# Turns of PSUM banks, mirrored value products and a new order of pairs in a fused attention and feed-forward kernel

## The chip, the cores and the metric

The kernel runs on one core of one Trainium2 chip. The time is the device time of one execution in microseconds (us). A number called "time" is the median of the undisturbed executions of one kernel; each batch of measurements ran the kernel before on the same chip in between. A number from a trace comes from one profiled execution and is counted from the start of its span.

Engines: PE is TensorE's matmuls, PEld its weight loads, DVE is VectorE, ACT is ScalarE, POOL is GpSimd. PSUM is the memory that TensorE writes its results to; the kernel uses it as a tile `ps` of eight banks of 512 columns. `xT` is the normalised result of attention, transposed, the input of stage 1. "L584" is line 584 of the kernel that was profiled, so one statement has different line numbers in different kernels.

## The reference

```python
# q, k, v: (8 batches, 8 heads, 576 tokens, 64); per head, softmax over a causal band
mask_plain = (rel >= 0) & (rel < 32)                          # heads 0..3
mask_dil = (rel >= 0) & (rel < 128) & (rel % 4 == 0)          # heads 4..7 ("dilated"; heads 0..3 are "plain")
attn = exp(scores - max) / (sum + 1e-09); attn_out = attn @ v
x = attn_out.transpose(0, 2, 1, 3).reshape(4608, 512)
g, val = x @ w_gate, x @ w_val                                # 512 -> 1536
out = (gelu(g) * val) @ w_out                                 # 1536 -> 512, fp32
```

## The kernel before

The 4608 tokens go through the feed-forward part in nine pieces (c = 0 to 8) of 512. Each piece has two stages. Stage 1 makes 12 pairs of PSUM banks, one for the gate and one for the values; ScalarE takes the gelu of the first, VectorE multiplies. Stage 2 makes four output blocks of 128 tokens, each the sum of 12 products in one bank, and ScalarE stores them. Attention is worked off two heads (a "pair" of heads, index n = 4 x batch + pair) at a time in between: scores (s), mask (m), value product (v), and the multiply by the reciprocal of the denominators (x); w is the last value product of a stage, in the banks of the scores. The string `places` says where each of these steps comes: "1.3v" is a value product in output block 1, counted from 0, after three of its twelve products.

ScalarE needs the exponential for the scores and gelu for stage 1. In the trace of the kernel before, each of the 13 changes between the two comes with a load of tables of 1283 ns (seven for gelu, six for the exponential). No source line asks for it: the compiler puts it in.

```python
    def ffn1_two(c, pairs):              # first two bank pairs of a piece
        for kc in range(NKC):            # NKC = 4: one kc for each pair of heads
            for nb in range(2):
                ...                      # gate and value product of this kc
        for nb in range(2):
            geglu(nb, pairs[nb])

    def geglu(nb, b0):
        g = ffn.tile([P, CH], F16, tag="g")        # a pool of three g buffers
        nc.scalar.activation(g, ps[:, b0, :], AF.Gelu)
        nc.vector.scalar_tensor_tensor(u_all[:, nb, :], g, USCALE, ps[:, b0 + 1, :], ALU.mult, ALU.mult)
    ...
    places = {
        1: "0.0m 1.2v 1.2x 1.2s 1.2m 1.12s 2.1v 2.1x 2.1m 2.12s 3.1v 3.1m 3.1x 3.12w 3.12x",
        ...                              # pieces 2 to 5
    }
    ...
            for tb in range(4):          # stage 2
                ...
                bank = mm0 + tb if not lone else first if tb == 0 else mm0
                ffn2(c, tb, bank, hooks)
                store(c, tb, bank, "dve" if c > 5 and tb == 3 else "act")
```

Scores take four of the eight banks, so a stage 2 with attention in it has the other four at hand (`mm0` to `mm0 + 3`): blocks 1 to 3 all use the bank `mm0`, so blocks 2 and 3 have to wait until ScalarE has stored the one before (2.2 us from 85 to 260 us, in seven waits of up to 0.3).

The softmax here doesn't subtract the row's maximum and nothing guards it: scores larger than these inputs give would overflow.

Of the kernel before, what the change touches and what calls it, by code (L numbers as in the profile page):

```python
# [17 lines left out]
USCALE = 32.0  # L18
# [20 lines left out]
def kernel(  # L39
# [211 lines left out]


    def is_plain(n):
        return n % NHP < NHP // 2

# [126 lines left out]

    def emit_pv(n, b0, parts=("den", "num"), wide=False):

# [16 lines left out]
        if is_plain(n):  # L401
            if "den" in parts:
                d0 = 1024 if wide else 960

                groups = (
                    ((0, 0, 4, P), (P, P, 3, 32), (PH - PT, 512, 1, PT))
                    if wide
                    else ((0, 0, 1, 64), (64, 64, 1, 64), (PW, P, 3, P), (P, P, 3, 32), (PH - PT, 512, 1, PT))
                )
                for i, (p0, q0, runs, w) in enumerate(groups):  # L410
                    for hl in range(2):
                        st = i == 0 or i == (2 if wide else 1)
                        add(hl, d0 + q0, [[P, runs], [1, w]], ones[:, 0:D], hl * PH + p0, [[PW, runs], [1, w]], st)
            if "num" in parts:
                for j in range(5):
                    for hl in range(2):
                        lhs = vp[:, j, hp, 2 * hl, :] if j < 4 else vt[:, hp, 2 * hl, :]
                        w = (PW, PW, PW, P, PT)[j]
                        add(hl, j * P, run(w), lhs, hl * PH + j * PW - (32 if j == 4 else 0), run(w), j in (0, 4))
        else:  # L420
            if "den" in parts:

                groups = (
                    ((0, 0, DW, 1024), (1, 0, DW, 1536))
                    if wide
                    else ((0, 0, 192, 288), (0, 192, 96, 800), (1, 0, 96, 896), (1, 96, 192, 1312))
                )
                for i, (s, c, w, c0) in enumerate(groups):
                    for hl in range(2):
                        add(hl, c0, run(w), ones[:, 0:D], (2 * s + hl) * DW + c, run(w), wide or i != 2)  # L430
            if "num" in parts:
                for s in range(2):
                    for m in range(3):
                        for hl in range(2):
                            h, p0 = 2 * hp + hl, (2 * s + hl) * DW
                            if m < 2:
                                add(hl, 512 * s + m * NCL, run(P), vd[:, h, 2 * m + s, :], p0 + m * NCL, run(P), m == 0)
                            else:
                                two = [[NCL, 2], [1, 16]]
                                add(hl, 512 * s + P, two, vr[:, h, s, :], p0 + P, two, False)  # L440
        for o, lhs, rhs, st in mms:
# [33 lines left out]
    def norm_both_x(n, b0):  # L475
        b, hp = divmod(n, NHP)
        rb = tiles.pop(("rb", n))
        for hl in range(2):
            half = slice(64 * hl, 64 * hl + 64)
            nc.vector.tensor_tensor(  # L480
                xT[hp][half, b * S : (b + 1) * S], both_rows(hl, b0, hl), rb[half], ALU.mult
            )

    def den_ap(n, b0, wide):

        if is_plain(n):
            c0, dims = (1024, [[1, S]]) if wide else (960, [[1, S]])
        else:
# [3 lines left out]

    def norm_r(n, b0, wide=False):
        dt = nrm.tile([P, 18, 32], F32, tag="dt", bufs=1)
        den = den_ap(n, b0, wide)
        dims = den.ap[1:]
# [5 lines left out]

    def recip(n, dt):
        rc = nrm.tile([P, 18], F32, tag="rc")
        nc.vector.reciprocal(rc, dt[:, :, 0:1].rearrange("p b c -> p (b c)"))
        rb = nrm.tile([P, S], F32, tag="rb", bufs=4)
        nc.vector.transpose(  # L507
            rb.rearrange("p (b c) -> p b c", c=32),
            bass.AP(tensor=rc.tensor, offset=rc.offset, ap=[rc.ap[0], [1, 18], [0, 32]]),
        )  # L510
        tiles["rb", n] = rb

    def norm_x(n, b0):
        b, hp = divmod(n, NHP)
        rb = tiles.pop(("rb", n))
        dst = xT[hp][:, b * S : (b + 1) * S]
        if is_plain(n):
            nc.vector.tensor_tensor(dst, psf[:, b0 * 512 : b0 * 512 + S], rb, ALU.mult)
        else:
            num = ps[:, b0 : b0 + 2, 0 : 2 * NCL].rearrange("p s (m i) -> p i m s", m=2)  # L520
            nc.vector.tensor_tensor(  # L521
# [5 lines left out]

    def ffn1(c, nb, b0):
        tok = slice(c * CH, (c + 1) * CH)
        ns = slice((nb % 4) * P, (nb % 4 + 1) * P)  # L530
        for gi, w in ((0, wg_t[nb // 4]), (1, wv_t[nb // 4])):
            for kc in range(NKC):
                nc.tensor.matmul(  # L533
                    ps[:, b0 + gi, :], w[:, kc, ns], xT[kc][:, tok], start=(kc == 0), stop=(kc == NKC - 1)
                )
        geglu(nb, b0)

    def ffn1_two(c, pairs):

        tok = slice(c * CH, (c + 1) * CH)  # L540
        for kc in range(NKC):
            for nb in range(2):
                ns = slice(nb * P, (nb + 1) * P)
                for gi, w in ((0, wg_t[0]), (1, wv_t[0])):
                    nc.tensor.matmul(  # L545
                        ps[:, pairs[nb] + gi, :],
                        w[:, kc, ns],
                        xT[kc][:, tok],
                        start=(kc == 0),
                        stop=(kc == NKC - 1),  # L550
                    )
        for nb in range(2):
            geglu(nb, pairs[nb])

    def geglu(nb, b0):
        g = ffn.tile([P, CH], F16, tag="g")
        nc.scalar.activation(g, ps[:, b0, :], AF.Gelu)  # L557
        nc.vector.scalar_tensor_tensor(u_all[:, nb, :], g, USCALE, ps[:, b0 + 1, :], ALU.mult, ALU.mult)  # L558

# [106 lines left out]
    for hp in range(2):  # L666
# [18 lines left out]


    places = {
        1: "0.0m 1.2v 1.2x 1.2s 1.2m 1.12s 2.1v 2.1x 2.1m 2.12s 3.1v 3.1m 3.1x 3.12w 3.12x",
        2: "0.0m 1.2v 1.2x 1.2s 1.2m 1.12s 2.1v 2.1x 2.1m 2.12s 3.1v 3.1x 3.1m 3.7s 3.12v 3.12x 3.12m",
        3: "0.0m 1.2v 1.2x 1.2s 1.2m 1.12s 2.1v 2.1x 2.1m 2.12s 2.12m 3.1v 3.1x 3.7s 3.7m",  # L690
        4: "0.0m 1.4s 1.12v 1.12x 1.12m 2.3s 2.12v 2.12x 2.12m 3.2s 3.2m 3.12s 3.12m",
        5: "0.0m 1.4s 1.4m 1.12v 1.12x 2.3s 2.3m 2.12s 2.12m 3.6s 3.6m",
    }
    places = {c: [(int(w[0]), int(w[2:-1]), w[-1]) for w in p.split()] for c, p in places.items()}
    late = None
    for c in range(NCH):
# [4 lines left out]
        s_list = list(scores.get(c, ()))  # L701
        pairs = (mm0, mm0 + 2)
        swap = int(c < 2 or late == "bank")
        SB = 4 - mm0
# [3 lines left out]
        for nb in range(NNB):  # L708
            if nb == 0 and c < 2:
                ffn1_two(c, (4, 6) if c == 0 else (6, 0))  # L710
            elif nb == 0 and late == "x":
                ffn1_two(c, pairs)
            elif nb > 1 or c > 2 and late != "x":
                ffn1(c, nb, pairs[(nb + swap) % 2])
            if pend is not None:
# [30 lines left out]

        def norm(n, b0):
            norm_r(n, b0)
            norm_x(n, b0)


        V = mm0 + 1

# [17 lines left out]
        else:  # L771
            todo = list(values_b.get(c, ()))
            lone = c in values_b
            first = pairs[(NNB - 2 + swap) % 2] + (pairs[(NNB - 2 + swap) % 2] == mm0)

            going = []

            def do(kind):
                if kind == "s":
# [3 lines left out]
                elif kind == "x":  # L783
                    norm_x(*going.pop(0))
                else:
                    n, bank = todo.pop(0), SB if kind == "w" else V
                    emit_pv(n, bank)
                    norm_r(n, bank)
                    going.append((n, bank))

            late = None
            for tb in range(4):
                at = [(fc, kind) for t, fc, kind in places.get(c, ()) if t == tb]
                hooks = {}
                for fc, kind in at:
                    if fc < NNB:
                        hooks.setdefault(fc, []).append(lambda kind=kind: do(kind))
                bank = mm0 + tb if not lone else first if tb == 0 else mm0
                ffn2(c, tb, bank, hooks)
                store(c, tb, bank, "dve" if c > 5 and tb == 3 else "act")  # L800
                for fc, kind in at:
                    if fc == NNB:
                        do(kind)
            if lone:

                late = "bank"
                if len(values_b[c]) > 2:
                    late = "x"
                    if c > 1:
                        mm0 = 4 - mm0  # L810
            while masks:
# [29 lines left out]
```

## Time and profile before

| | kernel before |
|---|---|
| time | 360.56 us (360.35 to 361.32, 4 runs) |
| span of the profiled run | 358.6 us |
| TensorE / VectorE / ScalarE busy | 95% / 56% / 41% |
| ScalarE's table loads for gelu | 7, of 1283 ns each |

The prediction shows how TensorE's waits are found. This is the timeline of the kernel before, at the change from piece 1 to piece 2. The columns of a timeline are the start (us), the duration (us), engine, line, operation, output<-input and shapes, count, and in brackets the idle time before it with what ended it.

```profile
105.69 0.60 ACT L575 ACTIVATE osb<-ps 128x512 f32<-128x512 f32 x1 [2.56 <-PE ps L564]
...
106.30 1.28 ACT L557 ACT_TABLE_LOAD   x1
...
110.24 1.09 ACT L557 ACTIVATE g<-ps 128x512 f16<-128x512 f32 x2 [2.66 <-PE ps L545]
...
110.89 1.02 PE L533 MATMUL ps<-xT,wg 128*128 128x512 f16 x4
```

The load runs at 106.30, right behind the last store (0.02 us after its end). ScalarE then stands 2.66 us until TensorE has the first gate bank ready. TensorE starts its third bank pair (L533) 0.65 after the gelu's start, only 0.20 us later than it could.

### The profile page before, as it was taken

How to read it: one execution, taken by the hardware profiler on the slowest of the kernel's cores; microseconds unless marked ns; L12 is line 12 of the kernel's file. 1: busy time of each engine (PE TensorE's matmuls, PEld its weight loads, DVE VectorE, ACT ScalarE, POOL GpSimd, SP SyncE). 2: the span in 40 equal slices, each digit the busy share in tenths (PEclk: the TensorE clock that was granted, in tenths of full speed). 3: DMA queues.
4: the chain of work that ended last, by engine and by line, in shares of the span. 5: the costliest groups of instructions: out<-in, count | busy, mean ns of one | idle time of the engine just before them, and what ended most of it. 6: DMA issues, size and time to landing. Idle time of an engine off the chain costs nothing.

```text
span 358.6 us, 5943 instructions
## 1 busy us (share of the span) xinstructions
PE 342.4 (95%) x2326; PEld 165.7 (46%) x2326; DVE 201.3 (56%) x306; ACT 145.3 (41%) x212; POOL 78.4 (22%) x110
## 2 busy tenths in 40 slices
PE   6789999999999999899999999999999999999995
PEld 2554454444444444344445444544454444444442
DVE  3575455843585447773768837993589514403320
ACT  1732346253643364435463366326643223323321
POOL 2580334540432323063003600140000000000000
PEclk9958999999999999999999999999999999999999
DMA  8999999999899899699139952794100020011002
GB/s 197 240 188 214 212 150 197 177 163 242 182 137 204 192 155 177 161 182 136 60 99 205 149 115 76 167 159 71 59 31 0 31 88 0 3 72 45 2 29 88
DMA packets 107291, 45.30 MB, mean 126 GB/s; under 512 B 83040, under 2 KB 102496, under 8 KB 107264
## 3 DMA queue, kind: packets, MB, share of 16 engines
q1 hardware_dynamic: 84272, 31.21, 39.9%
q0 software_dynamic: 21456, 12.01, 26.5%
q10 hardware_dynamic: 1536, 1.70, 2.1%
q8 instruction: 18, 0.29, 0.4%
q14 instruction: 9, 0.07, 0.1%
HBM read 40.13 MB, written 9.44 MB: 138 GB/s over the span
## 4 chain that ended last, share of the span: by engine, by line
PE 79%; DVE 11%; DMA 3%; ACT 3%; issue 2%; ACTq 0%; DVEq 0%
PE ps L533 42%; PE ps L564 24%; PE ps L442 5%; PE ps L545 4%; DMA xT<-in_k_dram 3%; DVE xT L521 2%; DVE dt L500 2%; DVE rb L507 2%; ACT osb L575 1%; DVE dt L470 1%; PE ps L339 1%; DVE u_all L558 1%; PE ps L369 1%; DVE xT L480 1%; DVE P L379 1%
## 5 line engine op out<-in xcount | busy, mean ns | idle before, releaser
L558 DVE SCALAR_TENSOR_TENSOR u_all<-g,ps 128x512 f16<-128x512 f16 x108 | 72.7, 684 | 78.6 <-PE ps L533 66.2
L557 ACT ACTIVATE g<-ps 128x512 f16<-128x512 f32 x108 | 63.6, 597 | 123.7 <-PE ps L533 109.6
L564 PE MATMUL ps<-wo,u_all 128*128 128x512 f16 x432 | 100.9, 380 | 2.3 <-ACT osb L575 2.2
L533 PE MATMUL ps<-xT,wg 128*128 128x512 f16 x392 | 100.6, 379 | 0.3
L533 PE MATMUL ps<-xT,wv 128*128 128x512 f16 x392 | 100.6, 379 | 0.0
L564 PEld LDWEIGHTS <-u_all 128*128 128x128 f16 x432 | 39.5, 98 | 45.0 <-issue 0.5
L533 PEld LDWEIGHTS <-wv 128*128 128x128 f16 x392 | 38.4, 98 | 46.2
L533 PEld LDWEIGHTS <-wg 128*128 128x128 f16 x392 | 37.4, 98 | 44.1 <-issue 1.4
L575 ACT ACTIVATE osb<-ps 128x512 f32<-128x512 f32 x33 | 19.7, 598 | 46.5 <-PE ps L564 46.5
L199 POOL CAST qp<-st 128x2048 f16<-128x2048 f32 x6 | 11.4, 1896 | 99.1 <-DMA st<-in_k_dram 55.7
L500 DVE STREAM_TRANSPOSE dt<-ps 128x576 f32<-128x576 f32 x25 | 19.5, 780 | 17.0 <-PE ps L442 16.9
L507 DVE STREAM_TRANSPOSE rb<-rc 128x576 f32<-128x576 f32 x32 | 24.9, 778 | 1.1
L371 ACT ACTIVATE P<-ps 128x1152 f16<-128x1152 f32 x16 | 18.1, 1128 | 11.4 <-PE ps L369 11.4
L349 ACT ACTIVATE P<-ps 128x960 f16<-128x960 f32 x16 | 15.5, 971 | 12.1 <-PE ps L339 12.1
L379 DVE TENSOR_TENSOR P<-P,mask_p 128x1344 f16<-128x1344 f16 x14 | 12.0, 864 | 10.8 <-ACT P L350 10.8
L521 DVE TENSOR_TENSOR xT<-ps,rb 128x576 f16<-128x576 f32 x16 | 17.8, 1124 | 0.3
L577 DVE TENSOR_SCALAR osb<-ps 128x512 f32<-128x512 f32 x3 | 2.1, 692 | 27.8 <-PE ps L564 27.8
L545 PE MATMUL ps<-xT,wg 128*128 128x512 f16 x40 | 16.1, 403 | 0.9 <-DVE xT L521 0.9
L442 PE MATMUL ps<-P,ones 128*64 128x192 f16 (+5 forms) x174 | 12.2, 255 | 4.1 <-DVE P L379 1.9
L545 PE MATMUL ps<-xT,wv 128*128 128x512 f16 x40 | 15.9, 398 | 0.0
L442 PEld LDWEIGHTS <-ones 128*64 128x64 f16 x174 | 7.5, 112 | 14.7 <-issue 13.0
L379 DVE TENSOR_TENSOR P<-P,mask_d 128x1152 f16<-128x1152 f16 x12 | 9.0, 751 | 5.5 <-ACT P L371 5.5
(83 smaller groups left out, 267.1 us busy)
## 6 DMA issues: line engine op xcount, KB each, us to landing
out_dram<-osb SPq DMA_DIRECT2D x36, 256.0 KB, 2.0
sv<-in_v_dram SPq DMA_DIRECT2D x40, 128.0 KB, 3.6
st<-in_q_dram SPq DMA_DIRECT2D x24, 128.0 KB, 3.0
st<-in_k_dram SPq DMA_DIRECT2D x24, 128.0 KB, 3.0
qd<-in_q_dram POOLq DMA_DIRECT2D x7, 256.0 KB, 5.2
qd<-in_k_dram POOLq DMA_DIRECT2D x7, 256.0 KB, 7.0
vd<-in_v_dram POOLq DMA_DIRECT2D x7, 256.0 KB, 7.1
wg<-in_moe_w_gate_dram POOLq DMA_DIRECT2D x3, 512.0 KB, 7.5
```

The costliest lines, as they stand in the source:

```text
L371: nc.scalar.activation(pt, ps[:, b0 : b0 + 4, 0:DW], AF.Exp, bias=0.0, scale=scale)
L379: nc.vector.tensor_tensor(pt, pt, mb, ALU.mult)
L442: nc.tensor.matmul(o, lhs, rhs, start=st, stop=True, skip_group_check=True)
L500: nc.vector.transpose(dst, den)
L507: nc.vector.transpose(rb.rearrange("p (b c) -> p b c", c=32), bass.AP(tensor=rc.tensor, offset=rc.offset, ap=[rc.ap[0], [1, 18], [0, 32]]),)
L521: nc.vector.tensor_tensor(dst.rearrange("p (i m s) -> p i m s", m=2, s=2), num, rb.rearrange("p (s m i) -> p i m s", s=2, m=2), ALU.mult,)
L533: nc.tensor.matmul(ps[:, b0 + gi, :], w[:, kc, ns], xT[kc][:, tok], start=(kc == 0), stop=(kc == NKC - 1))
L545: nc.tensor.matmul(ps[:, pairs[nb] + gi, :], w[:, kc, ns], xT[kc][:, tok], start=(kc == 0), stop=(kc == NKC - 1),)
L557: nc.scalar.activation(g, ps[:, b0, :], AF.Gelu)
L558: nc.vector.scalar_tensor_tensor(u_all[:, nb, :], g, USCALE, ps[:, b0 + 1, :], ALU.mult, ALU.mult)
L564: nc.tensor.matmul(ps[:, bank, :], u_all[:, fc, tb * P : (tb + 1) * P], wo_t[fc // 4][:, fc % 4, :], start=(fc == 0), stop=(fc == NNB - 1),)
L575: nc.scalar.activation(osb, ps[:, bank, :], AF.Copy, bias=0.0, scale=1.0 / USCALE)
```

## The change

Its intent is to remove TensorE's waits at the end of stage 2.

1. Output blocks take turns in two banks (`ends`), the outer ones of the four. Value products use the other three, and their layout is mirrored (`flip`) when the block has the upper outer bank.
2. New `places`: value product, scores, multiply and mask follow at the same product.
3. In batches 2 and 3 the plain pairs of heads come last (`pair`), and the first products of pieces 2 and 3 take xT in the order 2, 3, 0, 1; from piece 2 to piece 4 the products of the last pair stand in a group of their own.
4. The last reciprocal of the stage in pieces 1 and 2 is worked in two parts (`norm_parts`): first the tokens that the next piece needs.

```diff
+    def pair(n):
+        return (n + 2 * (n // NHP in (2, 3))) % NHP
...
+    def norm_parts(n, b0, at):
+        for q0, q1 in ((0, at), (at, S)):
+            ...                  # transpose, reciprocal, transpose, multiply of q0:q1
...
-                    ffn1_two(c, pairs)
+                    ffn1_two(c, pairs, (2, 3, 0, 1) if c in (2, 3) else range(NKC), True)
...
-        1: "0.0m 1.2v 1.2x 1.2s 1.2m 1.12s 2.1v 2.1x 2.1m 2.12s 3.1v 3.1m 3.1x 3.12w 3.12x",
+        1: "0.0m 1.3v 1.3s 1.3x 1.3m 2.5v 2.5s 2.5x 2.5m 3.0s 3.0m 3.6v 3.6x 3.12w",
...                               # pieces 2 to 5 likewise; emit_pv and norms take flip
-                bank = mm0 + tb if not lone else first if tb == 0 else mm0
+                bank = ends[tb % 2] if lone else mm0 + tb
                 ffn2(c, tb, bank, hooks)
```

In `geglu` only the way in which the two banks are named is changed.

## The prediction

> **What bounds the kernel now.** I read the page's busy shares first: TensorE 95% of a span of 358.6 us, VectorE 56%, ScalarE 41%. Then the page's chain of work that ended last:
>
> ```profile
> PE 342.4 (95%) x2326; PEld 165.7 (46%) x2326; DVE 201.3 (56%) x306; ACT 145.3 (41%) x212; POOL 78.4 (22%) x110
> PE 79%; DVE 11%; DMA 3%; ACT 3%; issue 2%; ACTq 0%; DVEq 0%
> ```
>
> TensorE sets the end, but a seventh of the chain is VectorE and ScalarE: places where TensorE stands and another engine finishes. The view of waits, TensorE only, 85 to 260 us (who waits for whom: us in total, times, longest), says where:
>
> ```profile
> PE ps L564 <- ACT osb L575: 2.2, 7, 0.3
> PE ps L442 <- DVE P L379: 1.9, 4, 0.8
> PE ps L545 <- DVE xT L521: 0.9, 2, 0.5
> PE ps L442 <- DVE xT L480: 0.3, 1, 0.3
> ```
>
> Three kinds: an output block (L564) waits for ScalarE to store the block before, as they share a bank; a product of values (L442) waits for the mask on its probabilities (L379); the first products of the next piece (L545) wait for the last normalised heads (L521). The modelled end of a matmul hides part of each, so I take losses from starts in the timeline. Piece 2 (512 tokens each, counted from 0), end of its second stage:
>
> ```profile
> 139.43 0.28 PE L369 MATMUL ps<-qTd 64*128 64x128 f16 x4
> 139.54 0.60 ACT L575 ACTIVATE osb<-ps 128x512 f32<-128x512 f32 x1 [2.64 <-PE ps L564]
> ...
> 140.19 0.38 PE L564 MATMUL ps<-wo,u_all 128*128 128x512 f16 x1 [0.32 <-ACT osb L575]
> 140.49 0.44 PE L442 MATMUL ps<-P,ones 128*64 128x192 f16 x8
> ...
> 143.18 1.13 DVE L521 TENSOR_TENSOR xT<-ps,rb 128x576 f16<-128x576 f32 x1
> ...
> 144.23 0.75 DVE L379 TENSOR_TENSOR P<-P,mask_d 128x1152 f16<-128x1152 f16 x1
> ...
> 145.03 0.44 PE L442 MATMUL ps<-P,ones 128*64 128x192 f16 x8 [0.84 <-DVE P L379]
> ...
> 147.74 1.13 DVE L521 TENSOR_TENSOR xT<-ps,rb 128x576 f16<-128x576 f32 x1
> ...
> 148.92 0.38 PE L545 MATMUL ps<-xT,wg 128*128 128x512 f16 x1 [0.48 <-DVE xT L521]
> ...
> 149.98 1.02 PE L533 MATMUL ps<-xT,wg 128*128 128x512 f16 x4
> ```
>
> The scores at 139.43 take 0.37 us undisturbed (172.19 to 172.56), so L564 was due at 139.80 and came at 140.19; with the switch of shape (0.09) it lost 0.47. The values at 145.03 lost 1.00 in the same way, the first products at 148.92 lost 0.64, the pair after it 0.20 (gelu has to empty the bank). Done for every place from 68 us on where a start comes over 0.15 us late, the sums are: pieces 1 to 5, second stage and start of the next piece, 2.7, 2.8, 1.7, 1.0, 0.7 us; first stages 1.1 (0.30 at 74.27, 0.47 at 236.75, 0.31 at 273.61). In all 9.9 us, of which the 1.1, and 0.2 per piece at the gelu, are not aimed at. The change can reach about 8.2 us, 2.3% of the time.
>
> [...]Here undisturbed 512-column starts lie 0.216 apart; I use that slot. [...]the transpose of the denominators begins only after the last value matmul (103.21 after a product from 102.46), though the denominators were written first. [...]the plain L518 took 0.757[...]. [...]the trace has 1283. The loads stay.
>
> **The change, part by part.** Durations: score block 0.40 plain, 0.37 dilated, 0.09 more when coming from a 512-column product; value product 0.72 plain, 0.65 dilated, same 0.09; transpose 0.78, reciprocal 0.27, second transpose 0.78, from value product's start to their end 2.7 with the wait; multiply into xT 0.67 plain or 1.05 dilated as a slot; mask to value product 0.80 (144.23 to 145.03), 0.90 plain.
>
> *(a) Turns of banks.* A block no longer shares the bank of the block before. The seven recorded waits (0.47 each, one 0.41), two of 0.19 (213.22, 251.31) and the 0.42 of a value product at 93.75 go: 4.1 us of the 8.2. What is added: value products start at the fourth product of block 1, and mirrored ones, or those beside them, touch the bank that the block before is still being stored from: about 0.1 in pieces 3, 4, 5.
>
> *(b) New places and order.* A value product, then scores, then multiply, then mask. The chain on VectorE from one dilated value product to the next is 0.78 + 1.93 + 1.05 + 0.80 = 4.56 us (212.46 to 217.07 measured: 4.61). TensorE has in between 0.65 + 0.37 + 14 x 0.216 + 0.09 = 4.1 in pieces 1 and 2, and 0.2 less in piece 4. So the mask wait is **not** removed, it becomes about 0.4 there and 0.65 in piece 4. From the second to the third value product the plain mask leaves 0.2 more. In piece 3 the first product is plain, its chain 0.4 shorter: waits of 0.1 twice.
>
> *(c) Plain pairs last, reciprocal in parts.* Counting from S, the first scores before the stage, piece 1: third value product at 12.9, VectorE then has the mask of the last pair and norms, multiply done at 16.5. TensorE ends the fourth value product at 15.7 and comes to the first product that needs this pair, now its third and no longer its ninth, at 16.2: a wait of 0.4. The first part (384 columns) [...]done at 18.6; TensorE is there at 18.7. So no wait. Next pair of banks after the gelu 1.06 later: 19.76. Before: 110.89 - 89.90 = 20.99. **Gain 1.2.** Piece 2 adds a plain score block (0.5) whose exp, 1.35 us long, still reads the banks the fourth value product needs (0.35). VectorE then has part one [...], part two [...], a mask (0.8), and only then the multiply after the gelu (0.69), which frees a bank: S + 21.85 for the second half of the next pair, so 20.99 for its first. Before: 149.98 - 128.25 = 21.73. **Gain 0.7.**
>
> *Piece 3*, by the same count: start of the next piece 15.1, next pair 18.74, before 187.80 - 167.92 = 19.88. **Gain 1.1.** *Piece 4*: second stage 14.70 long, but the next piece's second bank is now the last output block's, whose store queues behind an exp of 1.13 issued two products earlier: 0.5 more. 15.2 against 221.29 - 206.33 = 14.96. **Loss 0.2.** *Piece 5*: 13.4 against 258.32 - 244.40 = 13.92. **Gain 0.5.** Pieces 7 and 8: the second bank of the first pair is the last block's, and VectorE's store takes 0.69: 0.08 each. **Loss 0.2.** Pieces 0, 6, and the loads are as before: dilated keys of batch 2 are in at 78 us, wanted at 90.
>
> Sum: 1.2 + 0.7 + 1.1 - 0.2 + 0.5 - 0.2 = 3.1; the wait at 236.75 may shrink by up to 0.3, as TensorE gets there later and VectorE doesn't. I take 3.3, that is **357.3 us** (0.9% faster).
>
> **Rivals.** *All waits go*: 8.2 us, 352.4. For it: the places are spread so that each mask is asked for a block before its use, and every block has a free bank. Against it: 4.56 us of chain against 4.1 of other work, which holds whatever bank the block is in; I give it 4%. *VectorE becomes the bound*: its work in 89.8 to 106.4 is 11.3 of 16.6, and splitting the last reciprocal adds three instructions[...], in piece 2 ahead of a mask and the gelu's multiply. If the second part always delays the next piece[...], the gains of pieces 1 and 2 vanish: 359.2. *A hidden conflict of banks in the mirrored layout* at every block, 0.3 each in 14 blocks, would leave 361.5; the first group of a mirrored product does lie in the bank being stored, but the store ends within 0.1 of its start.
>
> **Range and chances.** Each gain is a difference of two waits known to some 0.2; five pieces, partly common errors: 1 us either way, wider upward for rival two and downward for finer overlap. 355.2 to 359.0. Over 2% faster (below 353.4) would need 7.2 of the 8.2 us: 0.04. Over 2% slower: 0.01.
>
> **What would show it.** No wait of L564 for L575 in pieces 1 to 5. Waits for the mask left, about 0.4 and 0.2 in pieces 1 and 2 and 0.65 in piece 4. In piece 1 the first products halt at the third, by 0.4, and not at the last four. In piece 2 the second bank of the third pair starts late, behind VectorE. In piece 5 the second bank of its first pair waits 0.5 for a store. I am wrong if mask waits are gone, or if the waits for stores reappear under the value products.

The changed kernel's trace has, from the start of the first transpose to the end of the multiply, 2.04 us for 384 columns and 1.40 for the other 192 in piece 1 (from 106.60 and 108.56), 1.84 for 320 and 1.61 for 256 in piece 2 (from 145.57 and 147.32). "The trace has 1283" is the length of a table load in ns in the kernel before.

## The result, and the profile after

| | before | after |
|---|---|---|
| time, same rounds | 360.56 us (360.35 to 361.32, 4 runs) | 361.27 us (360.78 to 361.47, 4 runs) |
| ratio of the means, 95% interval | | 1.0014 (0.9996 to 1.0031): the same |
| span of the profiled run | 358.6 us | 359.4 us |

Ratios here and below are the mean time of one kernel's fast runs over the mean of the other's fast runs in the same rounds, so they are not quite the ratio of the medians quoted.

The prediction was 357.3, with a range of 355.2 to 359.0. The measured time lies above that range. Two views of the changed kernel's page first, the busy shares and the chain that ended last:

```profile
PE 338.7 (94%) x2326; PEld 164.2 (46%) x2326; DVE 204.4 (57%) x314; ACT 145.8 (41%) x212; POOL 78.4 (22%) x110
PE 66%; DVE 13%; DMA 13%; issue 3%; POOL 2%; ACT 1%; ACTq 0%; SPq 0%; DVEq 0%; POOLq 0%
```

TensorE executes as many matmuls as before, and VectorE has eight instructions more (314 against 306), as the change asks. Nothing in these two lines shows a new bound. The chain's larger share of DMA (13% against 3%) lies in the first 75 us throughout, in the first loads, and behind that no DMA is on it; there the chain was followed back another way than before. The view of TensorE's waits from 85 to 260 us says more (who waits for whom: us in total, times, longest):

```profile
PE ps L562 <- ACT g L584: 4.1, 3, 1.4
PE ps L455 <- DVE P L383: 2.4, 5, 0.9
PE ps L562 <- ACT osb L602: 0.3, 1, 0.3
PE ps L455 <- ACT P L354: 0.2, 1, 0.2
```

The seven waits of an output block for a store (2.2 us before) are gone; the wait for L602 in the third line is one of a stage 1 product (L562). In the first line there is something that the kernel before does not have at all: three times, TensorE's stage 1 (L562) stands 1.4 us for a gelu (L584). The view of groups by shape gives the matching line for the gelu loads. It shows what the loads cost, and after the second bar, how long ScalarE stood idle before them, for the kernel before (L557) and the changed one (L584):

```profile
L557 ACT ACT_TABLE_LOAD x7 | 9.0, 1283 | 3.4 <-PE ps L545 3.0 <-PE ps L533 0.3
...
L584 ACT ACT_TABLE_LOAD x7 | 9.0, 1283 | 12.4 <-PE ps L562 12.3
```

So the loads are as many and as long as before, but now they wait for TensorE. The timeline at the change from piece 1 to piece 2 shows how:

```profile
105.33 0.60 ACT L602 ACTIVATE osb<-ps 128x512 f32<-128x512 f32 x1 [2.38 <-PE ps L591]
...
109.35 1.28 ACT L584 ACT_TABLE_LOAD   x1 [3.42 <-PE ps L562]
...
110.64 1.08 ACT L584 ACTIVATE g<-ps 128x512 f16<-128x512 f32 x2
...
111.29 1.02 PE L562 MATMUL ps<-xT,wg 128*128 128x512 f16 x4 [1.38 <-ACT g L584]
```

ScalarE is free at 105.93, but the load starts only at 109.35, when TensorE has finished the first gate bank. Then the gelu has to wait 1.28 us for it, and with the gelu TensorE's third bank pair. That pair comes 1.54 us later than it could, against 0.20 before. The same happens at 150.38 and 188.53, at the start of pieces 3 and 4. The excess is 3 x 1.34 = 4.0 us. Predicted gain (3.3) minus 4.0 is a loss of 0.7; the medians show a loss of 0.7. That the two agree so well is partly luck: in the second measure that is used below the parts gain 2.8 and the loads cost 3.8.

**Where the load stands in the program.** The compiled program for ScalarE can be listed without running it. The rows around this place, before and after, with the engines that each instruction waits for:

```text
before   66 L575 Activation osb_1269<-ps_115 128x512 [waits DMAHW4_49,PE_49]
         67 L557 LoadActFuncSet
         68 L557 Activation g_1357<-ps_115 128x512 [waits PE_49]
after    66 L602 Activation osb_1269<-ps_115 128x512 [waits DMAHW4_49,DVE_49,PE_49]
         67 L584 LoadActFuncSet [waits PE_49]
         68 L584 Activation g_1364<-ps_115 128x512 [waits Activation_49]
```

In both, the load stands directly ahead of the gelu. What differs is where the wait for TensorE is. Before, the gelu has one wait and carries it itself, so the load ahead of it waits for nothing. After, the gelu has a second wait, on ScalarE's own earlier use of the g buffer (it is met by then: the last gelu of piece 1 ended at 89.32). It carries that one itself. The wait for TensorE goes into the program ahead of it, and the load behind that wait. The traces show the same: in the changed kernel a separate semaphore instruction of L584 runs on ScalarE at 109.30 and the load follows it at 109.35; in the kernel before none stands between the store, which ends at 106.28, and the load at 106.30.

### The profile page after: what moved, and what is told of

It is laid out like the page before. It is cut to its first block, busy times and chain, and to the rows that moved or that the text cites. A ratio compares the mean times of both kernels' runs of the same rounds, so it can differ in the third digit from the quotient of the medians.

```text
span 359.4 us, 5962 instructions
## 1 busy us (share of the span) xinstructions
PE 338.7 (94%) x2326; PEld 164.2 (46%) x2326; DVE 204.4 (57%) x314; ACT 145.8 (41%) x212; POOL 78.4 (22%) x110
## 4 chain that ended last, share of the span: by engine, by line
PE 66%; DVE 13%; DMA 13%; issue 3%; POOL 2%; ACT 1%; ACTq 0%; SPq 0%; DVEq 0%; POOLq 0%
PE ps L562 40%; PE ps L591 20%; PE ps L455 4%; DMA xT<-in_k_dram 4%; DMA st<-in_k_dram 3%; DMA wv<-in_moe_w_val_dram 3%; DMA wo<-in_moe_w_out_dram 2%; DVE P L383 2%; DVE xT L537 2%; DVE rb L522 2%; DVE dt L513 2%; DVE dt L483 2%; DVE u_all L585 2%; DVE xT L493 1%; DMA sv<-in_v_dram 1%
## 5 line engine op out<-in xcount | busy, mean ns | idle before, releaser
L562 PE MATMUL ps<-xT,wg 128*128 128x512 f16 x432 | 114.0, 379 | 5.1 <-ACT g L584 4.1
L562 PE MATMUL ps<-xT,wv 128*128 128x512 f16 x432 | 113.8, 379 | 0.3 <-ACT osb L602 0.3
L584 ACT ACTIVATE g<-ps 128x512 f16<-128x512 f32 x108 | 63.7, 597 | 116.8 <-PE ps L562 116.6
L562 PEld LDWEIGHTS <-wv 128*128 128x128 f16 x432 | 42.2, 98 | 52.7 <-issue 2.6
L562 PEld LDWEIGHTS <-wg 128*128 128x128 f16 x432 | 41.1, 98 | 52.5 <-issue 5.5
L602 ACT ACTIVATE osb<-ps 128x512 f32<-128x512 f32 x33 | 19.7, 598 | 38.1 <-PE ps L591 36.6
L513 DVE STREAM_TRANSPOSE dt<-ps 128x576 f32<-128x576 f32 x23 | 17.9, 780 | 14.5 <-PE ps L455 14.3
L522 DVE STREAM_TRANSPOSE rb<-rc 128x576 f32<-128x576 f32 (+4 forms) x34 | 25.3, 743 | 1.2
L455 PE MATMUL ps<-P,ones 128*64 128x96 f16 (+5 forms) x174 | 12.0, 253 | 5.0 <-DVE P L383 2.9
L383 DVE TENSOR_TENSOR P<-P,mask_p 128x1344 f16<-128x1344 f16 x14 | 12.4, 891 | 5.0 <-ACT P L354 4.9
L584 ACT ACT_TABLE_LOAD x7 | 9.0, 1283 | 12.4 <-PE ps L562 12.3
L483 DVE STREAM_TRANSPOSE dt<-ps 64x576 f32<-64x576 f32 x14 | 10.9, 781 | 0.4
```

The source lines that it names most:

```text
L383: nc.vector.tensor_tensor(pt, pt, mb, ALU.mult)
L455: nc.tensor.matmul(o, lhs, rhs, start=st, stop=True, skip_group_check=True)
L483: nc.vector.transpose(dt[64 * hl : 64 * hl + 64].rearrange("p b c -> p (b c)"), both_rows(1 - hl, b0, hl))
L513: nc.vector.transpose(dst, den)
L522: nc.vector.transpose(rb[:, 0 : 32 * nb].rearrange("p (b c) -> p b c", c=32), bass.AP(tensor=rc.tensor, offset=rc.offset, ap=[rc.ap[0], [1 ...
L562: nc.tensor.matmul(ps[:, bank, :], w[:, kc, ns], xT[kc][:, tok], start=first, stop=end)
```

## The experiments

To leave out the start-up (the third bank pair of piece 1 starts anywhere from 70.72 to 72.54 us in the eleven traces, and in after_early and early_turns, which run the same instructions up to there, at 71.44 and 72.43) a second measure is used: the **stretch** in the trace from the third bank pair of piece 1 to the first output product of piece 8. It is 344.07 - 72.24 = 271.8 us before, and 344.62 - 71.82 = 272.8 us after.

| run | time (lowest to highest, runs) | before, same rounds | ratio (95% interval) | stretch |
|---|---|---|---|---|
| after_early | 357.29 (356.77 to 357.74, 4) | 360.72 | 0.9909 (0.9882 to 0.9936) | 269.2 |
| before_late | 366.06 (365.64 to 367.09, 4) | 360.72 | 1.0157 (1.0128 to 1.0186) | 276.5 |
| early_whole | 357.96 (357.48 to 358.40, 5) | 360.72 | 0.9928 (0.9903 to 0.9952) | 269.6 |
| early_turns | 358.99 (358.15 to 359.24, 6) | 360.72 | 0.9949 (0.9924 to 0.9975) | 269.9 |
| early_masks | 356.43 (355.81 to 358.60, 6) | 360.72 | 0.9883 (0.9859 to 0.9908) | 270.0 |
| early_all | 357.69 (356.31 to 358.44, 6) | 360.72 | 0.9916 (0.9890 to 0.9942) | 268.9 |
| after_fresh | 357.51 (356.76 to 357.71, 4) | 360.64 | 0.9911 (0.9898 to 0.9924) | 269.0 |
| before_early | 360.70 (359.11 to 362.01, 6) | 360.64 | 1.0002 (0.9982 to 1.0022) | 271.8 |
| early_final | 355.29 (354.77 to 356.97, 5) | 360.64 | 0.9865 (0.9847 to 0.9884) | 266.9 |

The first four shared one set of rounds, the next two another, the last three a third. All results were correct.

### after_early: a gelu that waits for nothing

The changed kernel plus a gelu of one column, into a scratch buffer, right behind the last store of pieces 1, 2 and 3. The load comes with it.

```diff
+    junk = const.tile([P, 4], F16, tag="junk")
...
                 store(c, tb, bank, "dve" if c > 5 and tb == 3 else "act")
+                if tb == 3 and c in (1, 2, 3):
+                    nc.scalar.activation(junk[:, c - 1 : c], ones[:, 0:1], AF.Gelu)
```

> The changed kernel with one gelu of a single column put right behind the last store of pieces 1, 2 and 3, so that ScalarE loads its gelu table there and not behind its wait for TensorE. Theory (the load of 1.28 us went behind the wait for the first gate bank, and TensorE waits for it once in each of pieces 2, 3, 4): the three waits of 1.54 us fall to the 0.20 that they were before, 4.0 us less than the changed kernel, 357.3 us. Rival (VectorE is late with the second part of the reciprocal and the masks, the load would have fitted in anyway): 361 us as it is.

Measured: 357.29 us, against 361.27 of the changed kernel in its own rounds. The timeline of ScalarE at the same place:

```profile
104.63 0.60 ACT L603 ACTIVATE osb<-ps 128x512 f32<-128x512 f32 x1 [2.38 <-PE ps L592]
105.24 1.28 ACT L831 ACT_TABLE_LOAD   x1
106.54 0.20 ACT L831 ACTIVATE junk<-ones 128x1 f16<-128x1 f16 x1
108.66 1.09 ACT L585 ACTIVATE g<-ps 128x512 f16<-128x512 f32 x2 [1.92 <-PE ps L563]
```

The load is back behind the store (105.24), and the 4 us come back with it. This fits the theory, but an instruction has been added, so it doesn't yet prove why the load was late.

### before_late: the same loss, made in the kernel before

The kernel before plus a one-column copy of the first gate bank on ScalarE, ahead of the first gelu of pieces 2, 3 and 4. The copy waits for TensorE, and the load now follows it.

```diff
+        if c in (2, 3, 4):
+            nc.scalar.copy(junk[:, c - 2 : c - 1], ps[:, pairs[0], 0:1])
         for nb in range(2):
             geglu(nb, pairs[nb])
```

> The kernel before, with a copy of one column of the first gate bank put ahead of the first gelu of pieces 2, 3 and 4: ScalarE must wait for TensorE before it comes to its table load, as in the changed kernel, and nothing else of the change is in. Theory: 1.28 of load and some 0.2 of copy come on TensorE's path three times, 4.4 us, 365 us. Rival (what slows the changed kernel is the new order of values and masks): 360.6 us.

Measured: 366.06 us, 5.3 more than before; the stretch is 4.7 longer. TensorE's waits from 85 to 260 us:

```profile
PE ps L534 <- ACT g L560: 4.5, 3, 1.5
PE ps L443 <- DVE P L380: 1.9, 4, 0.8
```

The line of the changed kernel's loss appears in the old one, with nothing of the change in it. The third bank pair comes 1.67 us later than it could instead of 0.20, three times: 4.4 us. The copy's own 0.16 us is part of that. The stretch has 0.3 us more than these waits and the time 0.9; this remainder was not traced.

### after_fresh: only the second wait taken away

The decisive one: no instruction is added or moved. The first gelu of pieces 2, 3 and 4 (the 25th, 37th and 49th) writes a g buffer that nothing has used before. So it has no second wait.

```diff
     def geglu(nb, banks):
-        g = ffn.tile([P, CH], F16, tag="g")
+        gelus.append(nb)
+        fresh = len(gelus) in (25, 37, 49)
+        g = ffn.tile([P, CH], F16, tag=f"g{len(gelus)}" if fresh else "g", bufs=1 if fresh else 3)
```

The listing has changed as intended, with all else as in the changed kernel:

```text
         66 L606 Activation osb_1269<-ps_115 128x512 [waits DMAHW4_49,DVE_49,PE_49]
         67 L588 LoadActFuncSet
         68 L588 Activation g_1364<-ps_115 128x512 [waits PE_49]
```

> The changed kernel, where only the first gelu of pieces 2, 3 and 4 writes a g buffer of its own, never used before. No instruction is added or moved; the listing of the compiled program shows that the gelu then has one wait, for TensorE, which it carries itself, and that the table load ahead of it carries none. My theory (the load stood behind the wait for TensorE, because the gelu had a second wait and the first was moved ahead of the load): the loads run right behind the last store again, the third pair of banks waits some 0.2 us instead of 1.54 in these three pieces, and the time is 361.3 - 3 x 1.34 = 357.3 us, as with the added one-column gelu. Rival (the added one-column gelu helped in another way, by waking ScalarE or moving its queue): the waits of 1.54 us stay and the time is 361.

Measured: 357.51 us; the stretch is 269.0, 3.8 less than that of the changed kernel. The timeline:

```profile
104.38 0.60 ACT L606 ACTIVATE osb<-ps 128x512 f32<-128x512 f32 x1 [2.37 <-PE ps L595]
...
105.00 1.28 ACT L588 ACT_TABLE_LOAD   x1
...
108.35 1.08 ACT L588 ACTIVATE g<-ps 128x512 f16<-128x512 f32 x2 [2.07 <-PE ps L562]
...
109.00 1.02 PE L562 MATMUL ps<-xT,wg 128*128 128x512 f16 x4
```

The idle time before the seven loads is 3.4 us again, as in the kernel before. Where the wait stands relative to the load, and the buffer that is written, is all that differs, and it is worth the whole 3.8 us. The rival (the added gelu of after_early helped in another way) falls.

Simply giving the pool of g buffers 4, 5 or 6 places instead of 3 left the second wait in the listing, so more room alone is not what takes it away. These were built only, not run.

### before_early: a control

The kernel before, with the same added gelu as in after_early.

> A control: the kernel before with the same added one-column gelu right behind the last store of pieces 1, 2 and 3. There the loads already run ahead of the wait, right behind the store. My theory: nothing to win, the time stays within 0.3% of 360.6 us, and the third pair of banks waits 0.2 us as before. Rival (an early gelu is worth 4 us in any kernel, so the gain over the changed kernel has nothing to do with the change): 356.6 us.

Measured: 360.70 against 360.64, and the same stretch to 0.1 us. Where the load is early anyway, an early gelu wins nothing. So the gain of after_early is the repair of a loss that the change made, and is no gain that any version could have had.

### early_whole and early_turns: what the parts of the change are worth

Both start from after_early, so that the loads don't disturb. early_whole undoes the reciprocal in parts; early_turns also undoes the order of pairs and of the first products, so that only the turns of banks and the new places are left.

```diff
-                    norm_parts(n, SB, min(S, (c + 2) * CH - n // NHP * S))   # early_whole
+                    norm_r(n, SB)
+                    norm_x(n, SB)
...
-        return (n + 2 * (n // NHP in (2, 3))) % NHP                          # early_turns, in addition
+        return n % NHP
-                ffn1_two(c, pairs, (2, 3, 0, 1) if c in (2, 3) else range(NKC), True)
+                ffn1_two(c, pairs, range(NKC), False)
```

> As after_early, and the last reciprocal of pieces 1 and 2 whole again instead of in two parts. Theory: the last head pair is ready some 0.7 us later, of which TensorE has 0.2 to spare, so 0.5 us for each of two pieces, 1.0 us over after_early, 358.3 us. Rival (the three more VectorE instructions of the parts delay the masks and gelu multiplies): 0.5 us or more under after_early.

> As early_whole, and the pairs of batches 2 and 3 in their old order (plain first, dilated last), first products of the next piece taken head pair by head pair: of the change only the bank turns with their places are left. Theory: the dilated multiply is 0.4 longer, and it is the last one; the waits for the first products go back to about 0.6 a piece, 359 us. Rival (the new order is what costs): below early_whole.

Measured: 357.96 and 358.99 us. (A dilated multiply took 1.13 us and a plain one 0.75 in early_turns.) The reciprocal in parts wins 0.7 us by time and 0.4 by the stretch; the order of pairs and of the first products another 1.0 and 0.3. Each of the two is of the size of the spread, and only the sum, 1.7 us by time, is clear of it. The turns with the places win 1.7 of 360.7 (1.9 by the stretch). The first two lines of TensorE's waits from 85 to 260 us in early_turns show what the turns alone leave:

```profile
PE ps L563 <- DVE xT L538: 1.9, 3, 0.6
PE ps L456 <- DVE P L384: 1.3, 3, 0.6
```

No output block waits for a store any more, but there are 1.9 us of waits for the last multiply (L538), three times, where the kernel before has 0.9, twice. In the full after_early these are one short wait. So the turns deliver TensorE earlier at a multiply that VectorE has not done, and by time the second half of the change about doubles what the first half wins.

### early_all: an early gelu for piece 1 too

In every kernel so far, before as well, the first gelu of piece 1 has its load behind the wait, at a cost of 0.30 us. after_early plus one more early gelu, behind the last store of piece 0:

```diff
             store(c, 3, 1, "act")
+            nc.scalar.activation(junk[:, 3:4], ones[:, 0:1], AF.Gelu)
```

> As after_early, with the early gelu also behind the last store of piece 0, nothing else. The kernel before and the changed one both load the table for piece 1 behind the wait for TensorE, and lose 0.30 us there. Theory: that wait is cut, 0.3 us under after_early, 357.0 us. Rival: the wait of 0.30 is for the multiplies of the last values, no change.

Measured: 357.69 us (356.31 to 358.44). The 0.30 us is gone from the trace, but the time can't show it: its spread is 2.1 us, and the median is 0.4 above that of after_early, which is noise of the same kind. Inconclusive by time.

### early_masks and early_final: a version that beats both

What is left in after_early is mainly waits for masks. The early_masks version asks for the scores as soon as banks are free and does each mask ahead of its value product's turn on VectorE, with early_all's gelus:

```diff
-        1: "0.0m 1.3v 1.3s 1.3x 1.3m 2.5v 2.5s 2.5x 2.5m 3.0s 3.0m 3.6v 3.6x 3.12w",
+        1: "0.0m 0.9s 1.4m 1.4v 1.4x 1.6s 2.5m 2.5v 2.5x 2.8s 3.6m 3.6v 3.6x 3.12w",
...                               # pieces 2 to 5 likewise
```

> As after_early, one more early gelu for piece 1, and the places of scores and masks changed: each score block as soon as its banks are free, its mask before the value product ahead of it instead of behind that product's multiply. Theory (after the load, what is left are masks that VectorE takes up only after a chain of 4.56 us, and a store behind an exp in piece 4): the waits for masks in pieces 1 to 4 (0.8, 0.4, 0.7, 0.4, 0.3, 0.8), the two bank waits of 0.4 to 0.5 in pieces 2 and 5 and 0.3 at piece 1's gelu go, while the first products still wait for the last head pair: some 4 us under after_early, 353 us. Rival (VectorE is the bound in pieces 1 and 2 anyway, the waits only move to the first products): 356 us.

Measured: 356.43 us, where 353 was expected; the runs are spread over 2.8 us, and the profiled one, at 358.60, is the slowest. The two longest of TensorE's waits in the same window of that run:

```profile
PE ps L344 <- DMA qTp<-qp: 2.6, 1, 2.6
PE ps L563 <- DVE xT L535: 0.5, 2, 0.3
```

No wait for a mask is left, but one of 2.6 us for a load is new: the fifth scores of piece 2 are of batch 4, whose transposed plain keys were not yet in; the wait ends at 140.99. So at least in this run a gain was lost to a hidden transfer. The fastest run took 355.81 us and has no trace, so how long the others waited for the load is not shown.

In early_final, batch 4 has its dilated pairs first as well, as their keys land earlier (in early_masks the copy `kTr` that completes them ends at 132.46), and the masks left over at the end of a stage are put behind the first multiplies of the next piece. The order 2, 3, 0, 1 now holds for piece 4 too, and `places` of pieces 2, 3 and 5 shift a little.

```diff
-        return (n + 2 * (n // NHP in (2, 3))) % NHP
+        return (n + 2 * (n // NHP in (2, 3, 4))) % NHP
...
-            while masks:
-                mask_next()
+            carry = list(masks)          # emitted behind the next piece's first multiply
+            masks.clear()
```

> The version with early gelus and later places of the masks, and the dilated pairs first in batch 4 as well, so that the fifth scores asked for in piece 2 need keys that land early[...]; the mask of these scores is put behind the first multiply of piece 3. My theory (the gain of the new places was eaten by a wait of 2.8 us for a load): that wait goes, the mask waits stay away, and the time is about 353.5 us. Rival (piece 2 is held by loads anyway, the next one arriving as late): a wait for a load of over 1.5 us shows up elsewhere in pieces 2 and 3 and the time is about 356.

Measured: 355.29 us, 1.35% below the kernel before by the ratio, and the best version, though still within 2%. TensorE's waits from 85 to 260 us:

```profile
PE ps L563 <- DVE xT L535: 0.5, 2, 0.3
PE ps L563 <- ACT g L585: 0.4, 1, 0.4
PE ps L456 <- DVE xT L538: 0.3, 1, 0.3
```

The wait for the load is gone and none has taken its place, so the rival falls; but 353.5 was expected, and 1.8 us are missing. Part of it is probably that I had counted waits only. In these places scores and value products stand apart. Where nothing waits, a dilated value product alone holds up the row of 512-column products for 0.74 us (at 93.02) and dilated scores alone for 0.47 (at 91.04); one behind the other, as in the changed kernel, they do so for 1.11 (at 93.19). That saves 0.10 at each of nine places, an estimate of 0.9 us, half of what is missing. No run tests this alone, and the other half stays open. The trace is that of the fastest run (354.77), where early_masks has that of its slowest, so the two traces differ by more (3.1 us in the stretch) than the medians do (1.1).

## Why the prediction was wrong

**The step that failed** is in two short sentences of the prediction: "The loads stay", and "Next pair of banks after the gelu 1.06 later". I had seen 1283 ns for a table load in the trace, and taken its place in the order of ScalarE's program as given, because no line of the change touches it. The loads stayed in number and length, but in pieces 2, 3 and 4 they moved from the free side of a wait to the other. So the next pair came 1.34 us later than the sum said, three times. The view of groups by shape would have warned me to ask: before, only 3.4 us of idle time stood ahead of seven loads, nearly all of it in one place. Loads in ScalarE's free time were something to lose.

**With that one term put right, the sum held.** after_fresh is the changed kernel without it, and 357.51 us stands against the predicted 357.3. The stretch is 2.8 us shorter than before, where 3.3 was predicted. Its parts, from the first output product of a piece to the third bank pair of the next, in gains over the kernel before:

| piece | predicted | changed kernel | after_fresh |
|---|---|---|---|
| 1 | +1.2 | -0.85 | +0.7 |
| 2 | +0.7 | 0.0 | +0.9 |
| 3 | +1.1 | -0.3 | +1.0 |
| 4 | -0.2 | -0.3 | -0.3 |
| 5 | +0.5 | +0.5 | +0.5 |
| 6 and 7, into 7 and 8 | -0.2 | -0.2 | -0.2 |
| sum | 3.1 | -1.2 | 2.6 |

(After_fresh's piece 2 gains 1.3 up to the third pair; 0.45 of it is given back at 148.06, where the second bank of that pair waits for VectorE, and this is subtracted. The wait at 236.75, for which the prediction added 0.2, shrank by 0.15 in both.)

**Point by point:**

- *(a) Turns of banks.* Right. Output blocks wait for no store any more; the page's line for these products, before and after, has 2.3 and 0.1 us of idle time:

```profile
L564 PE MATMUL ps<-wo,u_all 128*128 128x512 f16 x432 | 100.9, 380 | 2.3 <-ACT osb L575 2.2
...
L591 PE MATMUL ps<-wo,u_all 128*128 128x512 f16 x432 | 100.3, 380 | 0.1
```

- *(b) The mask waits stay.* Right in kind, a little too small in size. From starts, less 0.09 for the switch of shape (in the kernel before, the scores at 89.90 start 0.31 behind the 512-column product ahead of them, where another such product starts 0.22 behind), the changed kernel loses 1.02 and 0.31 in piece 1, 0.48 and 0.28 in piece 2, 0.09 and 0.19 in piece 3, and 0.70 at the end of piece 4; predicted were 0.4 and 0.2, 0.4 and 0.2, 0.1 twice, and 0.65. The one large miss is the first of piece 1. There the mask itself took 1.29 us and not 0.75:

```profile
97.01 1.29 DVE L383 TENSOR_TENSOR P<-P,mask_d 128x1152 f16<-128x1152 f16 x1
97.14 1.24 POOL L218 DMA_DIRECT2D vr<-in_v_dram  x2
```

  In the other runs with this order the mask at this place took 0.74 (early_whole) to 1.13 (early_all), so it differs from run to run. GpSimd is at work beside the slow one, but in early_whole it is too, beside one of 0.74. No run separates its instructions, and what slowed the mask stays open. It is also most of why piece 1 gains 0.7 in after_fresh (mask 1.08 us) and not 1.2.
- *(c) The order of pairs and the parts.* Right, but for piece 1's mask. At the start of piece 2 the first products halt at the third one, by 0.35 (predicted 0.4), and not at the last four. The fourth value product of piece 2 waits for the exponential of the plain scores by 0.41 less the switch (predicted 0.35); the product starts 0.06 after the second half of the exponential has ended:

```profile
144.12 0.48 ACT L354 ACTIVATE P<-ps 128x384 f16<-128x384 f32 x1
...
144.66 0.49 PE L455 MATMUL ps<-P,ones 128*64 128x64 f16 x10 [0.25 <-ACT P L354]
```

  The multiply after the gelu that VectorE does late was predicted to free the bank 21.85 us after the stage's first scores. In after_fresh the product that needs it starts after 148.06 - 126.36 = 21.70. In the changed kernel itself this can't be seen, because the late load leaves VectorE time to catch up.
- *The loss in piece 4* was predicted as 0.5 for a store queued behind an exponential. It is there, 0.47:

```profile
221.52 1.13 ACT L375 ACTIVATE P<-ps 128x1152 f16<-128x1152 f32 x1 [1.08 <-PE ps L373]
...
222.54 0.59 ACT L602 ACTIVATE osb<-ps 128x512 f32<-128x512 f32 x1
...
223.19 1.02 PE L562 MATMUL ps<-xT,wv 128*128 128x512 f16 x4 [0.31 <-ACT osb L602]
```

- *The rivals.* The hidden conflict of banks was put at 361.5, which is nearly the measured 361.27, and is wrong all the same: no output block waits for a store, and after_fresh has the same mirrored layout and 357.5 us. A time that fits a theory doesn't confirm it; the wait that it names has to be in the trace. VectorE as the bound would have left 359.2; after_fresh runs in 357.5, and without the two parts of the reciprocal (early_whole) the time is no shorter, so they don't cost time. (They add four VectorE instructions in each of two pieces, 314 against 306, and not three as the prediction has it.) That all waits would go, needed the masks earlier; early_masks then found the next limit, a load, behind them.
- *The signs to watch* named in the prediction came out in kind, with two exceptions: one mask wait in piece 1 was 1.02 and not 0.4, and the late second bank in piece 2 shows only in after_fresh. None of them pointed to the loads, and yet the time was wrong. They covered only the places that the change aims at. A list of signs should have one for the rest: "no wait that isn't in the list of before".

**What stays open.** Why the compiled program gives the first gelu a second wait in the changed kernel and not before is not shown. The rows above have one more difference, that the store ahead of it now waits for VectorE too (DVE_49 in its row); no run tests whether that is the cause.

## What to carry to other kernels

A table load is not in the source, but it has a place in ScalarE's order, and a wait ahead of it can take it from free time onto the path, as here three times for 1.34 us each: after each change, compare the idle time in front of the loads (here 3.4 us became 12.4), and if it has grown, call the function once on one column where the engine is free anyway (after_early: 357.29 us against 361.27), or give that activation a buffer without history (after_fresh: 357.51). When a change fails to pay, look first for a wait that the kernel before doesn't have, and take it out alone before doubting the parts of the change: here the parts together were worth nearly what was predicted (2.6 of 3.1 us in the trace).
